# Where the fifth values and the fifth output weights travel in a decode block's stream of weights

## The chip, the cores and the metric

One core of a Trainium2 chip runs the whole program. The time is the device time of one execution, in microseconds; the kernel before took 214.63 us (median of 3 runs, 214.52 to 214.64).

## The reference

The program computes one decode step of a transformer block for a batch of B = 4 tokens of width D = 448, in float32:

```python
x_n = layernorm(x)                                   # (4, 448)
q = x_n @ wq                                         # 16 heads of 256
# 8 key/value groups, 2 heads each; the last W = 1024 cached positions
p = softmax(q . k_cache[:, g, -1024:, :] / 16)       # per token and head
o = p . v_cache[:, g, -1024:, :]
h = x + o.reshape(4, 4096) @ wo
y = layernorm(h)
out = h + gelu(y @ w1 + b1) @ w2 + b2                # w1: 448 x 1792
```

Keys and values of a group are 4 MB each, the query and output weights of a group 0.9 MB each, w1 and w2 3.2 MB each: about 88 MB that are read once, with little arithmetic on each byte.

## The kernel before, in words

**The stream.** Everything large is read by DMAs that SP issues into a ring of three slots of SBUF (pool `ring`, line 72). The list `LOADS` (lines 40 to 53) says what lies in each load, in order: quarters of keys and of values (2048 columns of 128 partitions each), query weights and output weights (1792 columns each). A load is one DMA with one semaphore, so nothing in it can be used before all of it has landed, and its slot is free for the load three places later when its last reader is done. `part` (line 89) issues the next load when a piece that isn't there yet is asked for. Behind the twelve loads come values 7 in two DMAs (`load_v7`, line 123), output weights 6 and 7, w1 and w2 (lines 351 to 360), in slots of the same ring. The program is written so that SP waits for slots, not for PE's place in the program.

**A group.** For group g of 8, `project_q` (line 196) makes the queries: products into PSUM, a copy to SBUF by ACT, and then products that both transpose and fold the four partition quadrants, since the four chunks of the contraction stand in four quadrants (`sel` has a one for each; two copies by DVE spread the result into `qT`). `scores` (214) multiplies queries and keys and takes the softmax's maximum (DVE) and exponentials (ACT). `transpose_p` (242) transposes the weights, and `values` (254) multiplies them with the values, a quarter at a time: 8 PE records of the 32. `heads` (274) scales the result, half on DVE and then half on ACT, transposes it and picks the rows of the two heads (`rows_of_pair`), and `project_o` (293) multiplies with the output weights. Groups 0 to 5 add up in one PSUM bank `acc`; for the last two groups the sum continues in `hsum` in another layout, which starts with products of a copy `accs` of `acc` (lines 342 to 349).

**The order.** PE's instructions run in the order in which they are written (line 525); the other engines are ordered by the framework. In the loop (331 to 372) the scores of group g+1 and the queries of g+2 come ahead of the values of group g. `keep_warm(n)` (322) issues n products of zeros in bfloat16 with 512 columns, whose result nobody reads; they stand where PE would wait.

**The tail.** Lines 392 to 458: the sum h, its two means and variances, the up projection with w1 (`pu`), GELU, the down projection with w2 (`py`), whose last two DMAs are small, and the output. The rows x, b2 and b1 that are added there come in one small DMA from ACT's queue (line 169), 16 rows of 704 values.

**Start.** The first load has query weights 0, the transposed x (16 columns) and 48 columns of zeros.

Of the kernel before, what the change touches and what calls it, by code (L numbers as in the profile page):

```python
# [8 lines left out]
F32 = mybir.dt.float32  # L9
BF16 = mybir.dt.bfloat16  # L10
AF = mybir.ActivationFunctionType
ALU = mybir.AluOpType
AX = mybir.AxisListType
PSUM = bass.MemoryType.PSUM

B, D = 4, 448
HQ, HKV, SK, DH = 16, 8, 4096, 256
REP = HQ // HKV
W = min(4096, max(256, SK // 4))
F = 1792  # L20
P = 128
H = P // 2
ND = 4
NKC = W // P
NFC = F // P
FQ = F // 4
Q = 32
GAP = Q // B
KV = 8 * B * DH
WC = 4 * D  # L30
QU = KV // 4
X0 = 64
V7A = 6 * B * DH


def parts(kind, g, quarters=range(4)):
    return [(kind, g, i) for i in quarters]
# [8 lines left out]
    [*parts("v", 2, (3,)), ("o", 2, 0), *parts("k", 4), ("q", 5, 0)],  # L46
    [*parts("v", 3), ("o", 3, 0), *parts("k", 5, (0, 1))],
    [*parts("k", 5, (2, 3)), ("q", 6, 0), *parts("v", 4)],
    [("o", 4, 0), *parts("k", 6), ("q", 7, 0)],
    [*parts("v", 5), ("o", 5, 0)],  # L50
    [*parts("k", 7)],
    [*parts("v", 6)],
]


# [13 lines left out]
def block_kernel(ctx: ExitStack, tc, rows, first, streams, v7, wo67, w1, w2, out):  # L69
    nc = tc.nc  # L70
    const = ctx.enter_context(tc.tile_pool(name="const", bufs=1))
# [38 lines left out]
    def wo_rows(t):  # L110
        return t.rearrange("p (j e) -> p j e", j=4)
# [8 lines left out]
    def load_v(g, c):  # L120
        return part("v", g, c).rearrange("p (c b d) -> p c b d", c=2, b=B)
# [32 lines left out]
        nc.vector.tensor_scalar_mul(fold[3 * Q :, j, :], sel[3 * Q :, :], 0.5 / D)  # L154
    fold = fold.rearrange("p j q -> p (j q)")
    rows_of = ident.rearrange("p (j b e) -> p j b e", j=4, b=B)[:, :, :, 0]
    rows_of_pair = ident.rearrange("p (b q) -> p q b", b=B)
    qT = [const.tile([P, 2, B, Q], F32, name=f"qT{i}") for i in range(2)]
    pT = [const.tile([P, NKC // 2, B, Q], F32, name=f"pT{i}") for i in range(2)]
    oT = [const.tile([P, 4, Q], F32, name=f"oT{i}") for i in range(2)]  # L160
# [3 lines left out]
    for t in qT + oT + pT + [gT]:  # L164
        nc.gpsimd.memset(t, 0.0)

    rs = const.tile([P, 2 * P + FQ], F32, name="rs")
    nc.gpsimd.memset(rs, 0.0)
    nc.scalar.dma_start(rs[::GAP, :], rows)

    def spread(t):
        return t[..., ::GAP]
    xb, b2b, b1b = rs[:, :P], rs[:, P : 2 * P], rs[:, 2 * P :]


    def column_mean(t, name):
# [19 lines left out]
    def project_q(g, parts):  # L196
        pq = ps_m.tile([P, 512], F32, tag="m", name=f"pq{g}")
        for j, a, cols, w in parts:
            nc.tensor.matmul(pq[j * Q : (j + 1) * Q, cols], yT[:, a, :], w, start=True, stop=True)  # L199
        qs = work.tile([P, 512], F32, tag="qs", name=f"qs{g}")  # L200
        nc.scalar.copy(qs, pq)  # L201

        pt = ps_m.tile([P, 512], F32, tag="m", name=f"pqt{g}")
        if g == HKV - 1:
            keep_warm(3, pt)
        pt = pt[:, : 2 * REP * B].rearrange("p (a b) -> p a b", b=B)
        for i in range(2 * REP):
            nc.tensor.matmul(pt[:, i, :], qs[:, i * P : (i + 1) * P], sel[:, :B], start=True, stop=True)  # L208

        src = pt.rearrange("p (r c) b -> p c b r", r=REP)  # L210
        for i in range(2):
            nc.vector.tensor_copy(qT[g % 2][:, :, :, i * REP : (i + 1) * REP], src)  # L212

    def scores(g):
        s = [ps_s.tile([P, 512], F32, tag="s", name=f"s{g}_{h}") for h in range(2)]
        if g == HKV - 1:
            keep_warm(12, s[0])
        mx = work.tile([P, 2], F32, tag="mx", name=f"mx{g}")
        for h in range(2):
            for c in range(2):  # L220
                for b in range(B):
                    nc.tensor.matmul(  # L222
                        s[h][b * Q : (b + 1) * Q, :], qT[g % 2][:, c, b, :], load_k(g, h, c)[:, b, :],
                        start=(c == 0), stop=(c == 1),
                    )
            nc.vector.reduce_max(mx[:, h : h + 1], s[h], axis=AX.X)  # L226
        nm = work.tile([P, 1], F32, tag="nm", name=f"nm{g}")
        nc.vector.tensor_max(nm, mx[:, 0:1], mx[:, 1:2])
        nc.vector.tensor_scalar_mul(nm, nm, -SCALE)  # L229
        p = work.tile([P, 2 * 512], F32, tag="p", name=f"p{g}")  # L230
        sums = work.tile([P, 2], F32, tag="sums", name=f"sums{g}")
        for h in range(2):
            nc.scalar.activation(  # L233
                p[:, h * 512 : (h + 1) * 512], s[h], AF.Exp, bias=nm, scale=SCALE,
                accum_out=sums[:, h : h + 1],
            )
        rec = work.tile([P, 1], F32, tag="rec", name=f"rec{g}")
        nc.vector.tensor_add(rec, sums[:, 0:1], sums[:, 1:2])
        nc.vector.reciprocal(rec, rec)
        return p, rec  # L240
# [13 lines left out]
    def values(g, v7=None):  # L254
        po = ps_o.tile([P, 2, DH], F32, tag="o", name=f"po{g}")
        for c in range(NKC // 2):
            vt = load_v(g, c) if v7 is None else v7[c]
            for b in range(B):
                nc.tensor.matmul(  # L259
                    po[b * Q : (b + 1) * Q], pT[g % 2][:, c, b, :], vt[:, :, b, :],  # L260
                    start=(c == 0), stop=(c == NKC // 2 - 1),
                )
        return po
# [5 lines left out]
    def columns(t, j):  # L269
        if j < 3:  # L270
            return t[:, j * P : (j + 1) * P].rearrange("p (i c) -> p i c", i=2)
        return t[:, None, 3 * P :].to_broadcast([t.shape[0], 2, H])

    def heads(g, po, rec):
        o = work.tile([P, 2, DH], F32, tag="o", name=f"o{g}")
        nc.vector.tensor_scalar_mul(o[:, :, :P], po[:, :, :P], rec)  # L276
        nc.scalar.mul(o[:, :, P:], po[:, :, P:], rec)  # L277
        pt = ps_m.tile([P, 512], F32, tag="m", name=f"pot{g}")
        if g >= HKV - 3:
            keep_warm(3, pt)  # L280
        pt = pt[:, : 2 * REP * B].rearrange("p (c r b) -> p c r b", c=2, r=REP)
        for c in range(2):
            for i in range(2):
                nc.tensor.matmul(  # L284
                    pt[:, c], o[:, i, c * P : (c + 1) * P], rows_of_pair[:, i * REP : (i + 1) * REP, :],
                    start=(i == 0), stop=(i == 1),
                )
        if g >= HKV - 2:
            keep_warm(1)
        dst = oT[g % 2].rearrange("p (r c) q -> p c r q", r=REP)  # L290
        nc.vector.tensor_copy(spread(dst), pt)  # L291

    def project_o(g, wt):
        for i in range(4):
# [22 lines left out]
    nc.vector.tensor_mul(yT[H:, 4, :B], d[H:, 3, :], rx[H:, :])  # L317
    project_q(0, wq_parts(t0[:, :WC]))

    tail = []  # L320

    def keep_warm(n, to=None):
        to = tail[0][:, 0, :] if to is None else to
        for _ in range(n):
            nc.tensor.matmul(to[:Q, :512], idle[:, :Q], idle, start=True, stop=True)  # L325
# [5 lines left out]
    for g in range(HKV):  # L331
        if g + 1 < HKV:
            p, rec_next = scores(g + 1)
            if g + 2 < HKV:
                project_q(g + 2, wq_parts(part("q", g + 2)))
            transpose_p(g + 1, p)
            if g + 1 == HKV - 2:
                keep_warm(8, ps_m.tile([P, 512], F32, tag="m", name="wait"))
            if g + 1 == HKV - 1:
                keep_warm(2, ps_m.tile([P, 512], F32, tag="m", name="wait"))  # L340
                tail.append(ps_t.tile([P, 2, 512], F32, tag="t", name="tail"))
                accs = once.tile([P, D], F32, tag="u", name="accs")
                nc.scalar.copy(accs, acc)
                keep_warm(8)
                hsum = ps_s.tile([P, 512], F32, tag="s", name="hsum")[:, :P]
                ph = hsum.rearrange("p (i c) -> p i c", i=2)
                pu = ps_s.tile([P, 512], F32, tag="s", name="pu")[:, :FQ]
                for j in range(4):
                    nc.tensor.matmul(ph[j * Q : (j + 1) * Q], sel, columns(accs, j), start=True, stop=False)
        else:  # L350
            v7t = load_v7()
            tw = slot("w1")
            wo_last = [wo_rows(tw[:, i * WC : (i + 1) * WC]) for i in range(2)]
            nc.sync.dma_start(tw[:, : 2 * WC], wo67)
            tw1 = tw[:, 2 * WC : 2 * WC + W1C]
            for a, n in ((0, 2 * F), (2 * F, W1C - 2 * F)):
                nc.sync.dma_start(tw1[:, a : a + n], w1[:, a : a + n])
            tw2 = slot("w2")
            for c0, n in ((0, 8), (8, 3), (11, 2), (13, 1)):
                nc.sync.dma_start(tw2[:, c0 * D : (c0 + n) * D], w2[:, c0 * D : (c0 + n) * D])  # L360
        if g == HKV - 1:
            keep_warm(6)
        po = values(g, v7t if g == HKV - 1 else None)
        heads(g, po, rec)
        if g < HKV - 2:
            project_o(g, wo_rows(part("o", g)))
        if g == HKV - 1:
            keep_warm(3)
            for i in range(2):
                project_o(HKV - 2 + i, wo_last[i])  # L370
        if g + 1 < HKV:
            rec = rec_next
# [158 lines left out]
```

## Time and profile before

| | us |
|---|---|
| median of 3 runs | 214.63 (214.52 to 214.64) |
| the profiled execution | 214.54 |
| its span, first to last instruction | 212.8 |
| PE busy | 151.3 (71%) |
| PE weight loads busy | 66.6 (31%) |
| DVE busy | 33.5 (16%) |
| ACT busy | 24.0 (11%) |
| DMA mean rate over the span | 416 GB/s, 88.52 MB |
| mean granted TensorE clock | 0.856 |

The profile is of one execution. Busy shares are averages over the whole span; PE's records are pipelined and their ends modelled, so that a start tells more than a duration. A float32 product in the normal mode stands as two records and a transpose as one. In a row of the timeline the bracket is the idle time of that engine before the row and what ended it. The clock is the share of full speed that TensorE was granted: 1.00 is 2.4 GHz, 0.50 is 1.2 GHz.

### The profile page before, as it was taken

Reading aid. Unit: us, or ns where it says so; the run is one execution under the profiler, and the core shown is the slowest. Engines: PE = TensorE matmul, PEld = TensorE weight load, DVE = VectorE, ACT = ScalarE, POOL = GpSimd, SP = SyncE. Lnnn points to the kernel's source line nnn. Section 1 sums busy time; section 2 is a strip of 40 time slices with the busy share of each in tenths; the row PEclk is TensorE's granted clock in tenths of the full one; section 3 lists DMA queues with packets and bytes.
Section 4 is the critical chain, followed back from the end, with each engine's and each line's share of the span. In section 5 each row is a group of like instructions: output and inputs, shape, how many; then the busy total and the mean of one; then the engine's idle time right before and its main releaser. Section 6 shows DMA issues by size and latency. Waiting matters only on the chain.

```text
span 212.8 us, 2636 instructions
## 1 busy us (share of the span) xinstructions
PE 151.3 (71%) x1153; PEld 66.6 (31%) x1153; DVE 33.5 (16%) x138; ACT 24.0 (11%) x57; POOL 5.6 (3%) x17
## 2 busy tenths in 40 slices
PE   0476825842894896870798770687999999999994
PEld 0342311410421622330324130143352434436443
DVE  1410310400103001310104020031130031101230
ACT  1110200300002100210003000030030102000310
POOL 6100000000000000000000000000000000000110
PEclk9999985995558569997559996589699999999999
DMA  7899797999989899998999999999999999999992
GB/s 299 376 473 508 339 508 339 501 393 449 489 357 473 381 466 430 416 481 356 487 402 445 445 405 470 434 425 384 443 409 444 416 437 425 413 411 422 429 389 72
DMA packets 3355, 88.52 MB, mean 416 GB/s; under 512 B 384, under 2 KB 640, under 8 KB 1040
## 3 DMA queue, kind: packets, MB, share of 16 engines
q1 hardware_dynamic: 3312, 88.31, 96.9%
q8 instruction: 9, 0.15, 0.3%
q10 hardware_dynamic: 32, 0.05, 0.1%
q14 instruction: 2, 0.02, 0.0%
HBM read 88.29 MB, written 0.07 MB: 415 GB/s over the span
## 4 chain that ended last, share of the span: by engine, by line
DMA 79%; PE 17%; SPq 1%; DVE 1%; issue 0%
DMA stream<-stream 68%; DMA w<-w 11%; PE s L222 8%; PE po L259 4%; PE acc L296 2%; PE pot L284 2%; PE pq L199 1%; PE py L453 0%; DVE o L276 0%; SPq L97 0%; SPq L360 0%; DVE oT L291 0%; SPq L95 0%; DVE res L457 0%
## 5 line engine op out<-in xcount | busy, mean ns | idle before, releaser
L222 PE MATMUL s<-stream,qT 128*32 128x512 f32 x256 | 41.3, 796 | 18.5 <-DMA stream<-stream 18.5
L259 PE MATMUL po<-stream,pT 128*32 128x512 f32 x224 | 30.0, 675 | 16.0 <-DMA stream<-stream 16.0
L222 PEld LDWEIGHTS s<-stream,qT 128*32 128x32 f32 x256 | 10.6, 142 | 46.2 <-issue 33.8
L226 DVE TENSOR_REDUCE mx<-s 128x1 f32<-128x512 f32 x16 | 11.1, 692 | 64.1 <-PE s L222 64.1
L259 PEld LDWEIGHTS po<-stream,pT 128*32 128x32 f32 x224 | 6.8, 119 | 33.0 <-DMA stream<-stream 18.8
L199 PE MATMUL pq<-stream,yT 128*32 128x512 f32 (+1 forms) x80 | 10.7, 630 | 5.9 <-DMA stream<-stream 3.0
L208 PE MATMUL pqt<-sel,qs 128*128 128x4 f32 x64 | 10.1, 281 | 5.5 <-ACT qs L201 5.5
L201 ACT COPY qs<-pq 128x512 f32<-128x512 f32 x8 | 4.7, 585 | 77.5 <-PE pq L199 77.5
L284 PEld LDWEIGHTS pot<-ident,o 128*128 128x128 f32 x64 | 9.8, 225 | 10.9 <-DVE o L276 10.7
L284 PE MATMUL pot<-ident,o 128*128 128x8 f32 x64 | 10.8, 287 | 3.0 <-DVE o L276 3.0
L233 ACT ACTIVATE p<-s,nm 128x512 f32<-128x512 f32 x16 | 10.9, 688 | 17.7 <-DVE nm L229 17.7
L208 PEld LDWEIGHTS pqt<-sel,qs 128*128 128x128 f32 x64 | 9.4, 226 | 10.1 <-ACT qs L201 10.1
L276 DVE TENSOR_SCALAR o<-po,rec 128x256 f32<-128x256 f32 x8 | 3.9, 484 | 53.7 <-PE po L259 53.7
L277 ACT ACTIVATE o<-po,rec 128x256 f32<-128x256 f32 x8 | 3.8, 473 | 69.3 <-DVE o L276 69.3
L325 PEld LDWEIGHTS <-idle 128*32 128x32 bf16 x77 | 6.7, 96 | 10.2 <-issue 4.4
L247 PE MATMUL ppt<-ident,p 128*128 128x128 f32 x64 | 9.8, 299 | 0.0
L296 PE MATMUL acc<-stream,oT 128*32 128x448 f32 x48 | 7.5, 701 | 2.3 <-DVE oT L291 1.4
L199 PEld LDWEIGHTS pq<-stream,yT 128*32 128x32 f32 x80 | 4.4, 128 | 13.8 <-issue 12.8
L325 PE MATMUL tail<-idle 128*32 128x512 bf16 x33 | 8.5, 381 | 0.0
L247 PEld LDWEIGHTS ppt<-ident,p 128*128 128x128 f32 x64 | 8.1, 162 | 0.9 <-ACT p L233 0.7
L193 POOL TENSOR_TENSOR r<-ve_r,mhalf 128x1 f32<-128x1 f32 x2 | 1.1, 546 | 192.0 <-DVE ve_r L192 192.0
L212 DVE COPY qT<-pqt 128x16 f32<-128x16 f32 x16 | 2.0, 170 | 18.9 <-PE pqt L208 18.9
(99 smaller groups left out, 72.5 us busy)
## 6 DMA issues: line engine op xcount, KB each, us to landing
stream<-stream SPq DMA_DIRECT2D x5, 7040.0 KB, 40.4
stream<-stream SPq DMA_DIRECT2D x2, 6912.0 KB, 39.7
stream<-stream SPq DMA_DIRECT2D x2, 4992.0 KB, 25.1
stream<-stream SPq DMA_DIRECT2D x2, 4096.0 KB, 24.1
stream<-stream SPq DMA_DIRECT2D x1, 5888.0 KB, 34.4
w<-w SPq DMA_DIRECT2D x2, 1792.0 KB, 23.1
v<-v SPq DMA_DIRECT2D x1, 3072.0 KB, 20.0
w<-wo SPq DMA_DIRECT2D x1, 1792.0 KB, 20.1
```

The source lines that it names most:

```text
L199: nc.tensor.matmul(pq[j * Q : (j + 1) * Q, cols], yT[:, a, :], w, start=True, stop=True)
L201: nc.scalar.copy(qs, pq)
L208: nc.tensor.matmul(pt[:, i, :], qs[:, i * P : (i + 1) * P], sel[:, :B], start=True, stop=True)
L222: nc.tensor.matmul(s[h][b * Q : (b + 1) * Q, :], qT[g % 2][:, c, b, :], load_k(g, h, c)[:, b, :], start=(c == 0), stop=(c == 1),)
L226: nc.vector.reduce_max(mx[:, h : h + 1], s[h], axis=AX.X)
L233: nc.scalar.activation(p[:, h * 512 : (h + 1) * 512], s[h], AF.Exp, bias=nm, scale=SCALE, accum_out=sums[:, h : h + 1],)
L247: nc.tensor.transpose(pt[:, c, :], p[:, c * P : (c + 1) * P], ident)
L259: nc.tensor.matmul(po[b * Q : (b + 1) * Q], pT[g % 2][:, c, b, :], vt[:, :, b, :], start=(c == 0), stop=(c == NKC // 2 - 1),)
L276: nc.vector.tensor_scalar_mul(o[:, :, :P], po[:, :, :P], rec)
L284: nc.tensor.matmul(pt[:, c], o[:, i, c * P : (c + 1) * P], rows_of_pair[:, i * REP : (i + 1) * REP, :], start=(i == 0), stop=(i == 1),)
L296: nc.tensor.matmul(acc[i * Q : (i + 1) * Q, :], oT[g % 2][:, i, :], wt[:, i, :], start=(g == 0), stop=(g == HKV - 3),)
L325: nc.tensor.matmul(to[:Q, :512], idle[:, :Q], idle, start=True, stop=True)
```

## The change

Four things change together.

- **Loads.** The first quarter of values 5 goes to the end of the load with output weights 4, keys 6 and query weights 7. The other three quarters go into one load with keys 7. Output weights 5 come behind values 6. There are eleven loads for twelve, with the same bytes; the largest has 14336 columns for 14080.
- **PE's order with it.** Between the first and the second quarter of values 5 stand 28 keep-warm products. Output projection 5 moves from behind heads 5 to behind values 6, ahead of heads 6, and the copy `accs` with the first products of `hsum` from ahead of values 6 to behind heads 6. Other keep-warm runs change: 12 to 4 ahead of scores 7, 8 gone ahead of values 5, 6 to 4 ahead of values 7, 3 gone in heads 6, 3 to 5 ahead of the last output projections.
- **Parity sums.** In `project_q` and `heads` the products with `sel` and `rows_of_pair` become plain transposes with `ident`, and the sum over the quadrants (or over the two heads' halves) is a `tensor_reduce` on DVE that reads PSUM.
- **Small rows.** x and b1 are no longer read as rows. b1 comes transposed in 16 columns of the first load, in place of the zeros (32 columns behind the weights instead of 64); x and b1 are brought into rows on the chip with five transposes and some copies behind `project_q(0)`. b2 alone is read as rows, in two DMAs of 64 columns.

```diff
-X0 = 64
+X0 = 2 * ND * B
 ...
-    [("o", 4, 0), *parts("k", 6), ("q", 7, 0)],
-    [*parts("v", 5), ("o", 5, 0)],
-    [*parts("k", 7)],
-    [*parts("v", 6)],
+    [("o", 4, 0), *parts("k", 6), ("q", 7, 0), *parts("v", 5, (0,))],
+    [*parts("v", 5, (1, 2, 3)), *parts("k", 7)],
+    [*parts("v", 6), ("o", 5, 0)],
...
-    rs = const.tile([P, 2 * P + FQ], F32, name="rs")
-    nc.gpsimd.memset(rs, 0.0)
-    nc.scalar.dma_start(rs[::GAP, :], rows)
+    b2b = const.tile([P, P], F32, name="b2b")
+    nc.gpsimd.memset(b2b, 0.0)
+    for cols in (slice(0, H), slice(H, P)):
+        nc.scalar.dma_start(b2b[::GAP, cols], rows[:, cols])
+    rs = const.tile([P, P + FQ], F32, name="rs")
...
         for i in range(2 * REP):
-            nc.tensor.matmul(pt[:, i, :], qs[:, i * P : (i + 1) * P], sel[:, :B], start=True, stop=True)
+            nc.tensor.transpose(pt[:, i * P : (i + 1) * P], qs[:, i * P : (i + 1) * P], ident)
+        q = work.tile([P, 2 * REP, B], F32, tag="q", name=f"q{g}")
+        quadrants = pt.rearrange("p (i j q) -> p i q j", i=2 * REP, j=4)
+        nc.vector.tensor_reduce(q, quadrants[:, :, :B, :], axis=AX.X, op=ALU.add)
...
         if g == HKV - 1:
-            keep_warm(12, s[0])
+            keep_warm(4, s[0])
...
         for c in range(NKC // 2):
+            if g == HKV - 3 and c == 1:
+                keep_warm(28, ps_m.tile([P, 512], F32, tag="m", name="wait"))
...
-        if g >= HKV - 3:
+        if g in (HKV - 3, HKV - 1):
             keep_warm(3, pt)
...
-                nc.tensor.matmul(
-                    pt[:, c], o[:, i, c * P : (c + 1) * P], rows_of_pair[:, i * REP : (i + 1) * REP, :],
-                    start=(i == 0), stop=(i == 1),
-                )
+                at = (2 * i + c) * P - i * REP
+                nc.tensor.transpose(pt[:, at : at + P], o[:, i, c * P : (c + 1) * P], ident)
...
-        nc.vector.tensor_copy(spread(dst), pt)
+        dst = oT[g % 2].rearrange("p (r c) (b e) -> p r (c b) e", r=REP, b=B)[..., 0]
+        src = pt.rearrange("p (i k q) -> p q k i", i=2, q=Q)[:, :REP]
+        nc.vector.tensor_reduce(dst, src, axis=AX.X, op=ALU.add)
...
+    nc.vector.tensor_copy(spread(zT), xT)
+    b1s = work.tile([P, 2 * 512], F32, tag="p", name="b1s")[:, : 4 * P]
+    nc.vector.tensor_copy(
+        b1s.rearrange("p (c j q) -> p c j q", c=4, j=4), b1T[:, :, :, None].to_broadcast([P, 4, 4, Q])
+    )
+    pb = ps_s.tile([P, 512], F32, tag="s", name="pb")
+    for c in range(3):
+        nc.tensor.transpose(pb[:, c * P : (c + 1) * P], b1s[:, c * P : (c + 1) * P], ident)
+    nc.tensor.transpose(pb[:, 3 * P : FQ], b1s[:H, 3 * P :], ident[:H, :H])
+    nc.scalar.copy(b1b, pb[:, :FQ])
+    px = ps_s.tile([P, 512], F32, tag="s", name="px")
+    nc.tensor.transpose(px[:, :P], zT.rearrange("p j q -> p (j q)"), ident)
+    nc.vector.tensor_copy(xb, px[:, :P])
...
-            if g + 1 == HKV - 2:
-                keep_warm(8, ps_m.tile([P, 512], F32, tag="m", name="wait"))
             if g + 1 == HKV - 1:
                 keep_warm(2, ps_m.tile([P, 512], F32, tag="m", name="wait"))
                 tail.append(ps_t.tile([P, 2, 512], F32, tag="t", name="tail"))
-                accs = ... hsum = ... pu = ...      # to behind heads 6
                 keep_warm(8)
...
         if g == HKV - 1:
-            keep_warm(6)
+            keep_warm(4)
         po = values(g, v7t if g == HKV - 1 else None)
+        if g == HKV - 2:
+            project_o(g - 1, wo_rows(part("o", g - 1)))
         heads(g, po, rec)
-        if g < HKV - 2:
+        if g < HKV - 3:
             project_o(g, wo_rows(part("o", g)))
+        if g == HKV - 2:
+            accs = ... hsum = ... pu = ...
         if g == HKV - 1:
-            keep_warm(3)
+            keep_warm(5)
```

## Rows read from the trace of the kernel before

**Rows 1.** The page's chain of work that ended last: shares of the span by engine

```profile
DMA 79%; PE 17%; SPq 1%; DVE 1%; issue 0%
```

**Rows 2.** A stretch: window, length, busy by engine, granted clock, DMA share, GB/s

```profile
2.00:209.00 207.00, 150.36 (x1132) 66.06 (x1132) 32.37 (x131) 24.04 (x57) 4.15 (x8) 0.85 1.00 427
```

**Rows 3.** Timeline of SP's queue: start, us from first issue to last, line, target

```profile
25.05 0.33 SPq L97 DMA_DIRECT2D stream<-stream  x1
...
146.41 10.01 SPq L97 DMA_DIRECT2D stream<-stream  x2
167.53 0.80 SPq L126 DMA_DIRECT2D v<-v  x2
...
183.97 3.90 SPq L360 DMA_DIRECT2D w<-w  x4
```

**Rows 4.** Timeline of PE and its weight loads, where a load is awaited

```profile
118.39 1.92 PE L259 MATMUL po<-stream,pT 128*32 128x512 f32 x16 [1.10 <-DMA stream<-stream]
...
135.04 3.64 PE L222 MATMUL s<-stream,qT 128*32 128x512 f32 x16 [8.27 <-DMA stream<-stream]
...
149.07 1.16 PE L296 MATMUL acc<-stream,oT 128*32 128x448 f32 x8 [0.94 <-DMA stream<-stream]
...
160.80 3.64 PE L259 MATMUL po<-stream,pT 128*32 128x512 f32 x32 [0.18 <-DMA stream<-stream]
...
170.53 3.64 PE L222 MATMUL s<-stream,qT 128*32 128x512 f32 x32 [0.49 <-DMA stream<-stream]
...
180.26 3.64 PE L259 MATMUL po<-stream,pT 128*32 128x512 f32 x32 [0.18 <-DMA stream<-stream]
...
194.35 1.95 PE L302 MATMUL hsum<-w,oT 128*32 128x128 f32 x64 [0.31 <-DMA w<-wo]
...
201.89 0.16 PEld L422 LDWEIGHTS pu<-w,zT 128*32 128x32 f32 x8 [0.23 <-DMA w<-w]
...
208.98 0.37 PEld L453 LDWEIGHTS py<-w,gT 128*32 128x32 f32 x16 [0.34 <-DMA w<-w]
209.56 0.16 PEld L453 LDWEIGHTS py<-w,gT 128*32 128x32 f32 x8 [0.21 <-DMA w<-w]
```

**Rows 5.** Timeline of PE at the first scores

```profile
17.64 6.48 PE L222 MATMUL s<-stream,qT 128*32 128x512 f32 x32 [1.83 <-DMA stream<-stream]
```

**Rows 6.** Stretches, columns as in rows 2, after two waits of PE

```profile
135.00:140.00 5.00, 4.95 (x26) 1.34 (x26) 1.01 (x3) 0.00 (x0) 0.00 (x0) 0.55 1.05 452
...
150.00:152.00 2.00, 2.00 (x16) 0.75 (x12) 0.00 (x0) 0.00 (x0) 0.00 (x0) 0.50 0.74 319
152.00:154.00 2.00, 2.00 (x16) 0.59 (x12) 0.50 (x1) 0.00 (x0) 0.00 (x0) 0.72 1.07 459
```

**Rows 7.** Timeline, group 6's transposed weights, and what follows values 5

```profile
157.70 1.09 PE L247 MATMUL ppt<-ident,p 128*128 128x128 f32 x8
...
158.83 0.29 DVE L251 COPY pT<-ppt 128x32 f32<-128x32 f32 x2 [0.36 <-PE ppt L247]
...
164.26 0.81 PE L325 MATMUL pot<-idle 128*32 128x512 bf16 x3
```

**Rows 8.** Timeline, output projection 5, copy of the sums, scaling in heads 7

```profile
166.51 0.96 PE L296 MATMUL acc<-stream,oT 128*32 128x448 f32 x8 [0.28 <-DVE oT L291]
...
167.28 2.75 PE L325 MATMUL s<-idle 128*32 128x512 bf16 x12
167.53 0.53 ACT L343 COPY accs<-acc 128x448 f32<-128x448 f32 x1 [1.97 <-PE acc L296]
...
191.36 0.48 DVE L276 TENSOR_SCALAR o<-po,rec 128x256 f32<-128x256 f32 x1 [5.45 <-PE po L259]
...
191.94 0.47 ACT L277 ACTIVATE o<-po,rec 128x256 f32<-128x256 f32 x1 [6.91 <-DVE o L276]
```

**Rows 9.** Timeline, keep-warm products between scores 7 and values 6

```profile
173.99 2.32 PE L325 MATMUL ppt<-idle 128*32 128x512 bf16 x10
...
177.96 1.68 PE L325 MATMUL tail<-idle 128*32 128x512 bf16 x7
```

More of the change, by code (lines that the diff above doesn't have):

```diff
@@ L156, in block_kernel @@
     rows_of = ident.rearrange("p (j b e) -> p j b e", j=4, b=B)[:, :, :, 0]
-    rows_of_pair = ident.rearrange("p (b q) -> p q b", b=B)
     qT = [const.tile([P, 2, B, Q], F32, name=f"qT{i}") for i in range(2)]
@@ L165, in block_kernel @@
         nc.gpsimd.memset(t, 0.0)
-    rs = const.tile([P, 2 * P + FQ], F32, name="rs")
-    nc.gpsimd.memset(rs, 0.0)
-    nc.scalar.dma_start(rs[::GAP, :], rows)
+    b2b = const.tile([P, P], F32, name="b2b")
[3 more added lines that the diff above has]
+    rs = const.tile([P, P + FQ], F32, name="rs")
     def spread(t):
         return t[..., ::GAP]
-    xb, b2b, b1b = rs[:, :P], rs[:, P : 2 * P], rs[:, 2 * P :]
+    xb, b1b = rs[:, :P], rs[:, P:]
     def column_mean(t, name):
@@ L205, in project_q @@
             keep_warm(3, pt)
-        pt = pt[:, : 2 * REP * B].rearrange("p (a b) -> p a b", b=B)
         for i in range(2 * REP):
-            nc.tensor.matmul(pt[:, i, :], qs[:, i * P : (i + 1) * P], sel[:, :B], start=True, stop=True)
-        src = pt.rearrange("p (r c) b -> p c b r", r=REP)
+            nc.tensor.transpose(pt[:, i * P : (i + 1) * P], qs[:, i * P : (i + 1) * P], ident)
+        q = work.tile([P, 2 * REP, B], F32, tag="q", name=f"q{g}")
+        quadrants = pt.rearrange("p (i j q) -> p i q j", i=2 * REP, j=4)
+        nc.vector.tensor_reduce(q, quadrants[:, :, :B, :], axis=AX.X, op=ALU.add)
+        src = q.rearrange("p (r c) b -> p c b r", r=REP)
         for i in range(2):
@@ L278, in heads @@
         pt = ps_m.tile([P, 512], F32, tag="m", name=f"pot{g}")
-        if g >= HKV - 3:
+        if g in (HKV - 3, HKV - 1):
             keep_warm(3, pt)
-        pt = pt[:, : 2 * REP * B].rearrange("p (c r b) -> p c r b", c=2, r=REP)
         for c in range(2):
             for i in range(2):
-                nc.tensor.matmul(
-                    pt[:, c], o[:, i, c * P : (c + 1) * P], rows_of_pair[:, i * REP : (i + 1) * REP, :],
-                    start=(i == 0), stop=(i == 1),
-                )
+                at = (2 * i + c) * P - i * REP
+                nc.tensor.transpose(pt[:, at : at + P], o[:, i, c * P : (c + 1) * P], ident)
         if g >= HKV - 2:
             keep_warm(1)
-        dst = oT[g % 2].rearrange("p (r c) q -> p c r q", r=REP)
-        nc.vector.tensor_copy(spread(dst), pt)
+        dst = oT[g % 2].rearrange("p (r c) (b e) -> p r (c b) e", r=REP, b=B)[..., 0]
+        src = pt.rearrange("p (i k q) -> p q k i", i=2, q=Q)[:, :REP]
+        nc.vector.tensor_reduce(dst, src, axis=AX.X, op=ALU.add)
     def project_o(g, wt):
@@ L318, in block_kernel @@
     project_q(0, wq_parts(t0[:, :WC]))
+    b1T = t0[:, WC + ND * B :].rearrange("p (c j) -> p c j", c=4)
+    nc.vector.tensor_copy(spread(zT), xT)
[11 more added lines that the diff above has]
+    nc.vector.tensor_copy(xb, px[:, :P])
     tail = []
@@ L341, in block_kernel @@
                 tail.append(ps_t.tile([P, 2, 512], F32, tag="t", name="tail"))
-                accs = once.tile([P, D], F32, tag="u", name="accs")
-                nc.scalar.copy(accs, acc)
                 keep_warm(8)
[L345 to L349, printed above, removed]
         else:
@@ L361, in block_kernel @@
         if g == HKV - 1:
-            keep_warm(6)
+            keep_warm(4)
         po = values(g, v7t if g == HKV - 1 else None)
+        if g == HKV - 2:
+            project_o(g - 1, wo_rows(part("o", g - 1)))
         heads(g, po, rec)
-        if g < HKV - 2:
+        if g < HKV - 3:
             project_o(g, wo_rows(part("o", g)))
+        if g == HKV - 2:
+            accs = once.tile([P, D], F32, tag="u", name="accs")
+            nc.scalar.copy(accs, acc)
+            hsum = ps_s.tile([P, 512], F32, tag="s", name="hsum")[:, :P]
+            ph = hsum.rearrange("p (i c) -> p i c", i=2)
+            pu = ps_s.tile([P, 512], F32, tag="s", name="pu")[:, :FQ]
+            for j in range(4):
+                nc.tensor.matmul(ph[j * Q : (j + 1) * Q], sel, columns(accs, j), start=True, stop=False)
         if g == HKV - 1:
-            keep_warm(3)
+            keep_warm(5)
             for i in range(2):
@@ L487 @@
     wo = np.asarray(A_wo).reshape(HKV, 4, P, D).transpose(0, 2, 1, 3).reshape(HKV, P, 4 * D)
-    first = np.concatenate([wq[0], xT, np.zeros((P, X0 - ND * B), np.float32)], axis=1)
+    b1 = np.zeros((4, 4 * P), np.float32)
+    b1[:, :FQ] = np.asarray(B_b1).reshape(4, FQ)
+    first = np.concatenate([wq[0], xT, b1.reshape(4, 4, P).transpose(2, 1, 0).reshape(P, 16)], axis=1)
     def part(kind, g, i):
@@ L511 @@
     b2 = np.concatenate([b2, b2[:, 3 * P :]], axis=1)
-    rows = np.concatenate([quadrants(xp), quadrants(b2), quadrants(np.asarray(B_b1).reshape(1, F))], axis=2)
-    rows = rows.reshape(4 * B, -1)
+    rows = quadrants(b2).reshape(4 * B, -1)
     arrays = {
```

## The prediction

> **What bounds the kernel now.** I read four views. First the chain of waits: the shares by engine put 79% on transfers [rows 1]; the reader should see that PE appears only as the piece between two transfers. Next the stretches: from 2 to 209 us the DMA engines are busy all the time (share 1.00) at 427 GB/s [rows 2]. So the end is set by the bytes, as long as the queue never runs dry. Third the SP queue: the late loads are issued over 10 us before the one ahead of them is through (146.41 for one whose turn comes near 160.8, 167.53 for one whose turn comes near 180.3) [rows 3, 4], so a few us of later slot release cost nothing. Last the timeline of PE, for where PE waits for a transfer and how long, since that is the slack that the change can eat [rows 4]: 0.18 us ahead of the values of group 6 (180.26), 0.31 ahead of the last output projection (194.35), 0.23 in the up projection (201.89), 0.34 and 0.21 in the down projection (208.98, 209.56). PE is thus nearly as late as the transfers all along the last 40 us. What matters is whether the new order makes PE later than they are.
>
> **The transfers.** The rows shrink from 16x704 to 16x128 values and the first load by 32 columns: 36.9 KB and 16.4 KB, 53 KB at 427 GB/s, 0.12 us less. One load fewer: 8192 columns take 9.73 us (160.80 to 170.53, 170.53 to 180.26) and 14080 take 16.65 (118.39 to 135.04) [rows 4]; 1.175 ns a column and 0.1 us a load solve both, PE's own lag included, so I allow 0 to 0.1 and take 0.03. The stream ends 0.15 us earlier, and if it still set the end the profiled execution would take 214.4 for its 214.54.
> The order within it: the ninth load gets a quarter of values 5, 2048 columns, 2.43 us by the rate above, so output weights 4 and keys 6 are seen at 149.07 + 2.43 - 0.12 = 151.4. Keys 7 now come with the rest of values 5 and without output weights 5 (1792 columns, 2.13 us): 170.53 - 2.13 - 0.12 = 168.3 for both. Values 6 with output weights 5 land at 180.1, as values 6 alone did.
> The Trainium skill prices a load otherwise. "DMA: Bandwidth & Descriptors" (Anatomy of one DMA) fits a fixed cost of about 2 us to each DMA; if that stood in the stream, one load fewer would bring 2 us. The 9.73 and 16.65 us show at most a tenth of it between queued loads.
>
> **The start.** Five transposes, a broadcast copy and three copies are added before the first scores, some 2.5 us of PE, DVE and ACT by their nearest rows (eight transposes 1.09, a copy 0.15 to 0.53 [rows 7, 8]). PE waits 1.83 us for keys 0 there [rows 5], which hides most of it. Uncovered, up to 1 us, it would delay the release of the first slot from 25.05 [rows 3], when two more loads of 16.65 each are queued: nothing.
>
> **The parity sums.** In every group four products of two passes become four one-pass transposes (half of the 1.09 of eight [rows 7]) and a copy becomes a DVE sum over 32 or 64 values, which no row shows. Its bounds are 0.15 (one of the two copies of 128x32, 0.29 together [rows 7]) and 0.48 (DVE's 128x256 [rows 8]); I take 0.25. Through group 4 this lies ahead of waits for loads. In the tail the transposes are in the sum below, and the sum on DVE ends, at 0.48 too, under the keep-warm products that follow.
>
> **PE from 151.4.** Before, PE goes from output projection 4 (149.07) to the transposed weights of group 6 (158.83 + 0.29 [rows 7]) in 10.1 us. Now the first quarter of values 5 follows (8 of 32 products; 32 free PE after 164.26 - 160.80 = 3.46, so 0.86), and 28 keep-warm products at 0.216 ((2.32 - 0.38)/9 [rows 9]), 6.05. From 151.4 this ends at 168.4, beside the landing at 168.3. But PE has then been idle for 3.8 us (the 0.94 of before [rows 4], 2.3 for the later load, 0.55 for the shorter transposes of heads 4), and the clock counts: after 149.07 it was granted 0.50 until about 153, after the pause of 8.27 before 135.04 it was granted 0.55 on average up to 140 [rows 6], that is the low level of 1.2 GHz for 4.4 us. Low stretches of 3 to 6 us after work resumes cost 0.5 less to 1 us more than the 2 us lost before. I take 0.3 more: values 5 go on at 168.7 (bounds 168.3, when the landing decides, and 169.4).
>
> **From there to the last output projection, all on PE's path:**
> - three quarters of values 5: 3.71 from first product to DVE's scaling (160.80; scaling 3.71 after it as 0.25 after PE is free), less 0.86: 2.85.
> - heads 5: DVE 0.48, then ACT 0.47, which starts 0.58 after DVE (191.36, 191.94 [rows 8]), then two transposes; PE is free 1.45 after DVE's start. Four keep-warm products 0.87. Scores 7 start at 168.7 + 5.2 = 173.9, where they started at 170.53: moving the values in front of them costs 3.4.
> - scores 7 to values 6: 170.53 to 177.96 [rows 4, 9] and eight keep-warm products, 9.16: values 6 at 183.0, the load long there (180.1).
> - values 6, output projection 5 (0.77, from 166.51 to 167.28 [rows 8]), heads 6, ACT's copy of the sums 0.53 [rows 8], which ACT runs after its half of heads 6, eight small products 0.54 and four keep-warm ones: 3.71 + 0.58 + 0.47 + 0.6 + 0.6 + 0.87 = 6.8. Values 7 at 189.8. (Output projection 5 lies under DVE's and ACT's scaling.) The copy of the sums and its products were done before beside a wait for a load; here PE waits for them.
> - values 7: 3.71, and heads 7 with one and five keep-warm products: 1.45 + 1.30. The last output projection starts at 196.3, where it started at 194.35: 1.95 later.
>
> **What the tail gives back.** After 194.35 PE waits 0.23 and 0.55 for weights [rows 4]; these 0.78 absorb part. The end comes 1.95 - 0.78 = 1.2 us later: 215.7 for 214.54. With the landing deciding at 168.3 it is 0.8 (215.3), with the clock's upper bound 1.9 (216.4). The median of the runs shown is 0.09 above the profiled execution, less than the working resolves; I put the time at 215.7.
> The queue doesn't add to this: the last values 7 are issued near 163 (the slot goes with the first quarter of values 5), w1 near 178 against a queue filled until 190, w2 near 188, 4 us later than at 183.97 [rows 3], against one filled until 201.9.
>
> **The rivals.**
> 1. Transfers still set the end: 214.4, not slower. The place is the last output projection; it decides if that starts by 195.1, that is if my 27.6 us from 168.7 are 1.2 too many, or 0.8 from 168.3. For it: every keep-warm run is filler, and two of the heads' steps rest on one overlap each that I read from single rows. Against: each of the six pieces is a row of the same shape.
> 2. A second low stretch of the clock between 184 and 195, where three keep-warm products of heads 6 and two-pass products are gone and PE waits for ACT twice. At the 3 us of the stretch after 150 [rows 6] half is lost, 1.5 us more: 217.2. Against: project and keep-warm products still fill most of it.
> The Trainium skill speaks for this one: "TensorE: Matmul & The Clock Gate" (Part 4: PE-mode transpose) says that transposes don't count as busy for the clock as matmuls do. No row before shows transposes alone; the eight at 157.70 stand at full clock among other work [rows 7].
> 3. Faster: rival 1's short PE path, 0.12 for the bytes, 0.1 for the load, and a stream whose other sizes run 0.2% quicker (0.4 us of 207): 213.9. Nothing in the rows points to the last. By the fixed cost that the Trainium skill's DMA page states it would be 212.5; the two spacings leave that next to nothing, and I count it within this rival.
>
> **How the numbers follow.** My forecast 0.60, rival 1 0.24, rival 2 0.11, rival 3 0.05. 0.2% (0.43 us) is about what a measurement of this kernel can tell from no change. Forecast and rival 2 are slower by more than that, but for the edge of the forecast's lower bound (0.02 taken off); rival 1 lies within it save for 0.04 on the fast side, so faster 0.09, same 0.22, slower 0.69. The range runs from rival 1 (214.3) to the forecast's upper bound and part of rival 2, 217.0; the forecast's own is 215.2 to 216.5.
>
> **What would show it.** Right: in the changed profile no PE wait for a transfer between 170 and the down projection; scores 7 start near 173.9, values 6 near 183, the last output projection near 196.3; the down projection runs through without a wait for weights while the last transfer lands near 209.4. Wrong: PE waiting for w2 at the end, as now; or the output projection on time because keys 7 and values 5 are seen well before 168.

## The result and the profile after

The changed kernel takes 215.06 us (median of 13 runs, 214.77 to 215.72) and the kernel before 214.59 (13 runs beside them, 214.44 to 214.75): a ratio of 1.0028, 95% interval 1.0021 to 1.0036. It is slower, by 0.5 us where 1.2 was forecast. The profiled execution took 215.35, with a span of 213.5; against the 214.54 of before that is 0.81 more. The runs spread over 0.95 us, those of before over 0.31.

The chain of waits, shares by engine, in the changed kernel (against [rows 1]):

```profile
DMA 59%; PE 35%; DVE 1%; ACT 1%; issue 1%; SPq 1%; ACTq 0%
```

PE's share has doubled. The same view in order of time (start, length, what) shows where:

```profile
112.24 38.85 DMA stream<-stream
151.23 1.72 PE acc L298 x8
152.95 5.08 PE s L224 x32
...
161.67 1.00 PE po L263 x8
162.66 5.81 PE wait L343 x27
168.47 2.85 PE po L263 x21
171.35 0.49 DVE o L280
171.93 0.48 ACT o L281
...
177.29 2.16 PE ppt L343 x10
...
207.52 3.30 PE py L472 x66
```

After the load with output weights 4, at 151.23, no transfer stands on the chain any more: it is PE's work, its keep-warm products among it, with short steps of DVE and ACT, to the down projection. In [rows 4] PE waited for a load at 160.80, 170.53, 180.26, 194.35, 201.89, 208.98 and 209.56; none of these waits is left.

The steps of the sum, in the timeline of PE, ACT and DVE in the changed kernel (where three records of a group stand ahead of the last keep-warm product and the rest behind it, I count from the start of the longer row):

```profile
168.52 1.94 PE L263 MATMUL po<-stream,pT 128*32 128x512 f32 x16
...
173.70 3.60 PE L224 MATMUL s<-stream,qT 128*32 128x512 f32 x29
...
182.85 3.60 PE L263 MATMUL po<-stream,pT 128*32 128x512 f32 x29
...
187.11 0.47 ACT L281 ACTIVATE o<-po,rec 128x256 f32<-128x256 f32 x1 [7.09 <-DVE o L280]
...
187.48 0.52 ACT L380 COPY accs<-acc 128x448 f32<-128x448 f32 x1
188.01 0.39 PE L343 MATMUL tail<-idle 128*32 128x512 bf16 x1
188.07 0.55 PE L385 MATMUL hsum<-accs,sel 128*32 128x128 f32 x8
...
188.45 0.81 PE L343 MATMUL tail<-idle 128*32 128x512 bf16 x3
...
189.31 3.60 PE L263 MATMUL po<-v,pT 128*32 128x512 f32 x29
...
195.78 1.91 PE L304 MATMUL hsum<-w,oT 128*32 128x128 f32 x58
...
197.78 0.29 DVE L414 SCALAR_TENSOR_TENSOR h<-hsum,rs 128x128 f32<-128x128 f32 x1 [3.00 <-PE hsum L304]
...
207.52 3.26 PE L472 MATMUL py<-w,gT 128*32 128x128 f32 x112 [0.39 <-issue]
210.84 0.29 DVE L476 TENSOR_TENSOR res<-py,hb 128x128 f32<-128x128 f32 x1 [3.20 <-PE py L472]
```

The reader should see the last row but one: 112 records of the down projection in one piece, with no wait for w2 in it. The same places of the tail in the kernel before:

```profile
196.37 0.29 DVE L395 SCALAR_TENSOR_TENSOR h<-hsum,rs 128x128 f32<-128x128 f32 x1 [3.07 <-PE hsum L302]
...
206.31 3.68 PE L453 MATMUL py<-w,gT 128*32 128x128 f32 x112 [0.39 <-DVE gT L445]
210.06 0.29 DVE L457 TENSOR_TENSOR res<-py,hb 128x128 f32<-128x128 f32 x1 [3.63 <-PE py L453]
```

And the stretches around the pause (columns as in [rows 2]):

```profile
148.00:150.00 2.00, 0.00 (x0) 0.00 (x0) 0.00 (x0) 0.00 (x0) 0.00 (x0) 0.83 1.05 455
150.00:152.00 2.00, 0.77 (x8) 0.29 (x12) 0.00 (x0) 0.00 (x0) 0.00 (x0) 0.50 1.06 459
...
154.00:156.00 2.00, 2.00 (x12) 0.46 (x8) 0.00 (x0) 0.00 (x0) 0.00 (x0) 0.50 1.06 459
156.00:158.00 2.00, 2.00 (x24) 0.70 (x20) 0.69 (x1) 0.00 (x0) 0.00 (x0) 0.97 0.96 410
158.00:196.00 38.00, 37.47 (x277) 15.68 (x266) 6.43 (x24) 5.22 (x13) 0.00 (x0) 1.00 0.98 418
```

The clock fell to 1.2 GHz in PE's pause ahead of 151.23, stayed there for 4.9 us of work, and was full from 156.1 to the end.

### The profile page after: what moved, and what is told of

Read it like the earlier page. It is cut to its first block, busy times and chain, and to the rows that moved or that the text cites. A ratio compares the mean times of both kernels' runs of the same rounds, so it can differ in the third digit from the quotient of the medians.

```text
span 213.5 us, 2547 instructions
## 1 busy us (share of the span) xinstructions
PE 148.9 (70%) x1103; PEld 58.4 (27%) x1103; DVE 36.2 (17%) x149; ACT 24.5 (11%) x58; POOL 5.1 (2%) x17
## 4 chain that ended last, share of the span: by engine, by line
DMA 59%; PE 35%; DVE 1%; ACT 1%; issue 1%; SPq 1%; ACTq 0%
DMA stream<-stream 59%; PE po L263 8%; PE s L224 8%; PE tail L343 3%; PE wait L343 3%; PE acc L298 2%; PE pot L288 2%; PE pu L441 2%; PE py L472 2%; PE ppt L249 1%; DVE o L280 1%; PE ppt L343 1%; PE hsum L304 1%; PE pq L199 1%; ACT o L281 1%
## 5 line engine op out<-in xcount | busy, mean ns | idle before, releaser
L263 PE MATMUL po<-stream,pT 128*32 128x512 f32 x224 | 31.2, 681 | 14.9 <-DMA stream<-stream 14.9
L263 PEld LDWEIGHTS po<-stream,pT 128*32 128x32 f32 x224 | 7.5, 120 | 30.9 <-DMA stream<-stream 16.9
L298 PE MATMUL acc<-stream,oT 128*32 128x448 f32 x48 | 8.4, 750 | 4.7 <-DMA stream<-stream 3.6
L249 PE MATMUL ppt<-ident,p 128*128 128x128 f32 x64 | 11.1, 303 | 0.2
L343 PEld LDWEIGHTS <-idle 128*32 128x32 bf16 x86 | 7.7, 96 | 11.3 <-issue 4.3
L288 PE MATMUL pot<-ident,o 128*128 128x128 f32 x32 | 7.7, 338 | 3.7 <-DVE o L280 3.1
L207 PE MATMUL pqt<-ident,qs 128*128 128x128 f32 x32 | 6.1, 323 | 5.6 <-ACT qs L201 5.6
L288 PEld LDWEIGHTS pot<-ident,o 128*128 128x128 f32 x32 | 3.6, 156 | 13.5 <-DVE o L280 10.9
L343 PE MATMUL wait<-idle 128*32 128x512 bf16 x30 | 6.8, 379 | 0.0
L207 PEld LDWEIGHTS pqt<-ident,qs 128*128 128x128 f32 x32 | 3.9, 159 | 10.2 <-ACT qs L201 8.5
```

The source lines that it names most:

```text
L207: nc.tensor.transpose(pt[:, i * P : (i + 1) * P], qs[:, i * P : (i + 1) * P], ident)
L249: nc.tensor.transpose(pt[:, c, :], p[:, c * P : (c + 1) * P], ident)
L263: nc.tensor.matmul(po[b * Q : (b + 1) * Q], pT[g % 2][:, c, b, :], vt[:, :, b, :], start=(c == 0), stop=(c == NKC // 2 - 1),)
L288: nc.tensor.transpose(pt[:, at : at + P], o[:, i, c * P : (c + 1) * P], ident)
L298: nc.tensor.matmul(acc[i * Q : (i + 1) * Q, :], oT[g % 2][:, i, :], wt[:, i, :], start=(g == 0), stop=(g == HKV - 3),)
```

## The experiments

Theory A is that of the prediction: the new order puts PE behind the transfers. Theory B: the sums on DVE, the transposes or the start cost the time. Theory C: the clock does. Ratios are to the kernel before, measured beside each.

**The parts apart.** e1 is the changed kernel with the loads, the order and the keep-warm runs of before:

```diff
-    [("o", 4, 0), *parts("k", 6), ("q", 7, 0), *parts("v", 5, (0,))],
-    [*parts("v", 5, (1, 2, 3)), *parts("k", 7)],
-    [*parts("v", 6), ("o", 5, 0)],
+    [("o", 4, 0), *parts("k", 6), ("q", 7, 0)],
+    [*parts("v", 5), ("o", 5, 0)],
+    [*parts("k", 7)],
+    [*parts("v", 6)],
...
```

> The parity sums and the small rows as in the changed kernel, with the loads, PE's order and the keep-warm runs of the kernel before. Theory A (the order makes PE late): the transfers set the end again, 0.15 us earlier than before, so a ratio to before of 0.999 (214.4), with PE waiting for the last piece of w2. Theory B (the sums, the DVE work or the start cost the time): 1.002 to 1.003 (215.1), as the changed kernel.

Measured: 214.44 (11 runs), 0.9995 (0.9987 to 1.0004). PE's weight loads wait for transfers again:

```profile
194.22 1.69 PEld L303 LDWEIGHTS hsum<-w,oT 128*32 128x32 f32 x64 [0.96 <-DMA w<-wo]
201.76 0.16 PEld L439 LDWEIGHTS pu<-w,zT 128*32 128x32 f32 x8 [0.23 <-DMA w<-w]
...
209.44 0.16 PEld L470 LDWEIGHTS py<-w,gT 128*32 128x32 f32 x8 [0.19 <-DMA w<-w]
```

The last piece of w2 is seen at 209.44 for 209.56, so the smaller rows and first load do save 0.1 us of stream. The sums, the transposes and the start alone do not slow the kernel: B falls.

e2 is the kernel before with the new loads, order and keep-warm runs alone, the opposite edit:

```diff
-    [("o", 4, 0), *parts("k", 6), ("q", 7, 0)],
+    [("o", 4, 0), *parts("k", 6), ("q", 7, 0), *parts("v", 5, (0,))],
...
+            if g == HKV - 3 and c == 1:
+                keep_warm(28, ps_m.tile([P, 512], F32, tag="m", name="wait"))
...
```

> The loads, PE's order and the keep-warm runs of the changed kernel, with the products by sel and rows_of_pair and the small rows of the kernel before. Theory A: slower than the changed kernel too, because heads 5, 6 and 7 keep two more records each on PE's path (0.22 each) and the stream is 0.12 later: 1.005 (215.7). Theory B: no slower than before, 1.000.

Measured: 215.69 (6 runs), 1.0059 (1.0047 to 1.0071), as A expects. The loads and the order cost 1.2 us by themselves; the sums and rows then give 0.6 back. Most of that is the transposes, which shorten the heads on a path that PE now sets: in e2's profile values 5 to scores 7, values 6 to values 7 and values 7 to the last output projection take 5.37, 6.64 and 6.64 us, in the changed kernel's 5.18, 6.46 and 6.47. In e1, where the transfers set the end, only the bytes saved could count.

**Filler on PE's path.** By filler I mean keep-warm products. e3 leaves out ten keep-warm products, e5 adds ten, at the same place ahead of values 6:

```diff
-                keep_warm(2, ps_m.tile([P, 512], F32, tag="m", name="wait"))
                 tail.append(ps_t.tile([P, 2, 512], F32, tag="t", name="tail"))
-                keep_warm(8)          # e3; in e5: 2 and 18
```

> The changed kernel without the ten keep-warm products between scores 7 and values 6. Theory A: they lie on PE's path, so the last output projection could start 2.16 us earlier (193.6) and waits for its weights again (landing 194.0); the transfers set the end: 0.9985 (214.3). Theory C (the clock): without filler the granted clock falls to 0.5 somewhere after 180 and the time is above 215.5 (1.004 or more).

> The changed kernel with ten more keep-warm products (18 for 8) ahead of values 6. Theory A: PE's path has no slack left behind them, so all of 10 x 0.216 shows at the end: 215.06 + 2.16 = 217.2 (ratio 1.0125), and the transfers land when they did. If the transfers or the waits for them set the end: 215.1 (1.003).

Measured: e3 214.27 (11 runs), 0.9988 (0.9979 to 0.9996); e5 217.98 (4 runs), 1.0163 (1.0147 to 1.0178). In e3 the waits for weights are back, the clock stays at 1.00 from 158 to 196 (no sign of C), and the last landings are the end:

```profile
194.07 1.69 PEld L304 LDWEIGHTS hsum<-w,oT 128*32 128x32 f32 x64 [0.54 <-DMA w<-wo]
...
209.28 0.16 PEld L470 LDWEIGHTS py<-w,gT 128*32 128x32 f32 x8 [0.20 <-DMA w<-w]
```

e5 came 0.8 over its expected 217.2. Its timeline says where:

```profile
169.00 2.74 PE L263 MATMUL po<-stream,pT 128*32 128x512 f32 x21
...
185.47 3.60 PE L263 MATMUL po<-stream,pT 128*32 128x512 f32 x29
...
198.41 1.91 PE L304 MATMUL hsum<-w,oT 128*32 128x128 f32 x58
```

Values 5 went on at 169.00 instead of 168.52, 0.48 later before the added products come; from there to values 6 it is 16.47 for 14.33, the ten products and next to nothing else. So against the profiled 215.35 it is 2.16 and 0.48, 217.99. The low stretch after 151 ended at 157.0 here, in the changed kernel's profile at 156.1. The four runs stood together there (217.92 to 218.19), above the longest run of the changed kernel with 2.16 added (217.88); why all four came out that late is not shown.

**The common landing.** e6 loads three quarters of values 5 and keys 7 as two DMAs into the same slot, and moves filler from values 5 to places where PE then waits:

```diff
+            if wanted[0] == ("v", 5, 1):
+                nc.sync.dma_start(t[:, : 3 * QU], src[:, : 3 * QU])
+                nc.sync.dma_start(t[:, 3 * QU : src.shape[-1]], src[:, 3 * QU :])
...
-                keep_warm(28, ps_m.tile([P, 512], F32, tag="m", name="wait"))
```

> The changed kernel with its ninth-but-one load (three quarters of values 5, then keys 7) as two DMAs into the same slot, each with its own semaphore, and the 28 keep-warm products taken out of values 5 (4 more ahead of scores 7, 10 more ahead of values 6, where PE now waits). Theory A: it is the common landing that makes PE late, so values 5 run through at 161.7, scores 7 start when keys 7 land (168.1, for 173.7), values 6 wait for their load (179.9), and the transfers set the end: 0.9985 (214.3). If the place of output projection 5 and of the copied sums is what costs: not below 1.002.

Measured: 214.47 (11 runs), 0.9996 (0.9988 to 1.0005). PE is back in time everywhere:

```profile
160.31 3.64 PE L265 MATMUL po<-stream,pT 128*32 128x512 f32 x32
...
168.03 3.64 PE L228 MATMUL s<-stream,qT 128*32 128x512 f32 x32 [0.64 <-DMA stream<-stream]
...
179.87 3.64 PE L265 MATMUL po<-stream,pT 128*32 128x512 f32 x32 [0.34 <-DMA stream<-stream]
...
193.97 1.95 PE L306 MATMUL hsum<-w,oT 128*32 128x128 f32 x64
```

Scores 7 start at 168.03 instead of 173.70, with output projection 5 and the copied sums where the change put them. The cause is that values 5 wait for keys 7 and scores 7 then wait for values 5. The 28 products taken out are not what held values 5: in e10 (below), with 12 of them, PE still waits for the load, over 5 us.

```profile
168.13 4.07 PE L263 MATMUL po<-stream,pT 128*32 128x512 f32 x24 [5.03 <-DMA stream<-stream]
```

**The copied sums.** In e11 the four products of `accs` (eight records, which the prediction and the expectation call eight products) come behind values 7, the copy itself where it was.

```diff
         po = values(g, v7t if g == HKV - 1 else None)
+        if g == HKV - 1:
+            hsum = ...; pu = ...
+            for j in range(4): nc.tensor.matmul(ph[...], sel, columns(accs, j), start=True, stop=False)
```

> The changed kernel with its eight products of the copied sums behind values 7 instead of ahead of them, so that PE doesn't wait for ACT's copy. Theory A: values 7 start 0.43 us earlier (the time from 188.0 to 188.4 in which PE issues them and waits), all on the path: 215.06 - 0.4 = 214.65 (1.0007). If the wait is hidden: 215.06 (1.0025).

Measured: 214.78 (11 runs, 214.61 to 215.59), 1.0012 (1.0004 to 1.0021), 0.3 of the expected 0.4 below the changed kernel's median. The intervals of the two just touch, and the profile gives the price:

```profile
182.53 3.60 PE L263 MATMUL po<-stream,pT 128*32 128x512 f32 x29
...
188.78 3.60 PE L263 MATMUL po<-v,pT 128*32 128x512 f32 x29
```

Values 6 to values 7 take 6.25 us for the changed kernel's 6.46: these products lay on the path and cost 0.21, half of the 0.43 expected. The rest of what this execution gained (214.82 for 215.35) was there before values 6, which start 0.32 sooner.

**The clock.** e4 fills PE's pause ahead of output projection 4; e9 is the same kernel again; e8 has 36 products for 28 in values 5 besides, e10 has 12.

```diff
+        if g == HKV - 4:
+            keep_warm(16, ps_m.tile([P, 512], F32, tag="m", name="wait"))
         if g < HKV - 3:
             project_o(g, wo_rows(part("o", g)))
...
             if g == HKV - 3 and c == 1:
-                keep_warm(28, ps_m.tile([P, 512], F32, tag="m", name="wait"))
+                keep_warm(36, ps_m.tile([P, 512], F32, tag="m", name="wait"))   # e8; e10: 12; e4, e9: 28
```

> The changed kernel with 16 keep-warm products in PE's pause of 3.6 us ahead of output projection 4. Theory A with the clock as its cause of spread: the clock stays at 1.0 through scores 6, the 28 keep-warm products end near 166, and values 5 go on when their load lands (168.1) in every run: 1.0015 (214.9), with a spread of 0.4 us where the changed kernel has 0.95. If the low clock after that pause plays no part: 1.0028 and the same spread.

Measured: 215.55 (7 runs), 1.0044 (1.0025 to 1.0063), and the spread grew to 1.55: three runs at 214.83 to 214.93, four at 215.55 to 216.38. The profiled execution took 214.92 as expected, but the expectation had no price for the pause of 1.56 us that PE then makes ahead of the landing at 168.1:

```profile
168.09 2.78 PE L263 MATMUL po<-stream,pT 128*32 128x512 f32 x24 [1.56 <-DMA stream<-stream]
```

Hence three more:

> The kernel with the filled pause once more, for another profile: if this execution takes 215.5 or more, a stretch of clock 0.50 between 168 and 196 (about 1 to 1.7 us lost) shows it; if it takes 214.9, the clock is 1.00 there.

> The pause ahead of output projection 4 filled as in the run before, and 36 keep-warm products for 28 in values 5, so that PE doesn't pause ahead of the landing at 168.1 either. Theory A with the clock as cause of the spread: the runs of the other kernel at 215.5 to 216.4 fell to a low clock after its pause of 1.6 us at 166.5; without a pause every run is near its best, 214.9 (1.0018), spread under 0.4. If the spread has another cause: 215.5 again, spread above 1.

> As the kernel with the filled pause, but with 12 keep-warm products for 28 in values 5, so that PE pauses for about 5 us ahead of the landing at 168.1 in every execution. If the clock makes the long runs of that kernel: the granted clock falls to 0.50 in this pause and stays there for 1.5 to 5 us of values 5 and heads 5, half of which shows at the end: 215.6 to 217.3 in every run, none at 214.9. If something else makes them: 214.9 in most runs again.

Measured: e9 214.99 (8 runs; five at 214.85 to 215.00, three at 215.97 to 216.53), 1.0043 (1.0023 to 1.0063), its profile again of one of the short ones. e8 214.92 (11 runs, 214.82 to 215.09), 1.0019 (1.0010 to 1.0028). e10 216.53 (4 runs, 216.26 to 217.04), 1.0099 (1.0084 to 1.0115). The stretches of e10, and then one of e8:

```profile
164.00:166.00 2.00, 0.00 (x0) 0.00 (x0) 0.00 (x0) 0.00 (x0) 0.00 (x0) 1.00 0.82 352
166.00:168.00 2.00, 0.00 (x0) 0.00 (x0) 0.00 (x0) 0.00 (x0) 0.00 (x0) 0.84 0.84 359
168.00:170.00 2.00, 1.87 (x12) 0.57 (x16) 0.00 (x0) 0.00 (x0) 0.00 (x0) 0.50 1.02 439
170.00:172.00 2.00, 2.00 (x20) 0.41 (x13) 0.00 (x0) 0.00 (x0) 0.00 (x0) 0.81 1.11 479
```

```profile
148.00:196.00 48.00, 47.22 (x352) 19.55 (x351) 7.12 (x25) 5.23 (x13) 0.00 (x0) 1.00 0.99 425
```

In e10 the clock is at 1.2 GHz from the end of the pause to about 170.8, for 2.6 us of values 5, half of which is 1.3, and its profiled execution is 1.34 over e4's (216.26 and 214.92). In e8 PE is busy almost without a gap, the clock is 1.00 from 148 to 196, and the spread is 0.27. So the pause is what brings the long runs of e4 and e9. That it does so by this low clock is what e10 makes likely, and not shown: no profile caught a long run, and the mean clocks on record, over whole executions, do not tell the two kinds apart (0.879 to 0.889 in the seven long runs, 0.880 to 0.888 in the eight others).

e8 also answers C for the change itself: without any low stretch between 148 and 196 the kernel still takes 1.0019 of the one before, so the low clock alone does not make it slower, though it may add to it.

## Why the prediction was right, and where it was off

- **Bound and mechanism: right.** With the stream as the end, e1, e3 and e6 stand at 214.27 to 214.47 (forecast 214.4); with the new order PE sets it. Rival 1 (not slower) did not happen, because the slack that [rows 4] show behind the last output projection is 0.78 us and PE came 1.4 late to it. The 215.06 lies in the range, but just under the 215.2 to 216.5 that the prediction gave to this forecast alone: the mechanism is the forecast's, but two of its steps were taken too long (below).
- **The transfers: right.** Output weights 4 were seen at 151.23 (forecast 151.4), keys 7 with values 5 at 168.1 in e4, e9 and e10, where PE waits for them (168.3).
- **The start and the parity sums: right.** PE still waits 0.85 us for keys 0; the DVE sums took 0.19 (32 values) and 0.22 (64 values), for the 0.25 taken and the copies' 0.19.
- **Values 5 to scores 7 and on to values 6: right.** 168.52 to 173.70 is 5.18 (forecast 5.2), 173.70 to 182.85 is 9.15 (9.16), values 7 to the last output projection 6.47 (6.46).
- **Start of values 5: off by 0.2** in the profiled execution (168.5 for 168.7). The allowance for the clock was of the right kind. Four profiles are of the same code up to there: with the clock full again at 155.4 (e3), 155.5 (e11), 156.1 (the changed kernel) and 157.0 (e5), values 5 went on at 168.14, 168.06, 168.52 and 169.00, the first two at the landing. e8, without the low stretch, stands at 214.92 where the bound with the landing deciding said 215.3.
- **Values 6 to values 7: mis-sized, with a wait that was not there.** I took 6.8, it was 6.46 (182.85 to 189.31). The prediction has PE wait for ACT's copy of the sums. The copy begins at 187.48, ahead of the end of the scaling's row (187.11 + 0.47), and is done at 188.00; PE comes to the keep-warm product ahead of the eight records of `hsum` at 188.01, so it does not wait. These eight cost 0.21 (e11), where the sum has 0.6 for them. This and the start make the last output projection 1.43 late (195.78) for 1.95.
- **What the tail gives back: mis-sized.** 1.41 us at the sum h (197.78 for 196.37) became 0.78 at the output (210.84 for 210.06): 0.63 given back for 0.78. The 0.23 of the up projection gave 0.21 (203.09 for 201.89), the 0.55 of the down projection only 0.42: without its two waits its row shrinks from 3.68 to 3.26, so not all of the idle time in such a bracket was lost.
- **Together** 1.43 - 0.63 = 0.8 in the profiled execution, for a forecast of 1.2; its 215.35 lies 0.29 over the median. A low stretch longer than in most runs would explain that; the other runs have no profile, so it is not shown.
- **Rival 2 (a second low stretch): did not happen.** The clock was 1.00 from 158 to 196. By the Trainium skill, "TensorE: Matmul & The Clock Gate" (Part 4: PE-mode transpose), transposes do not count as busy for the clock the way matmuls do. The trace does not contradict it: among other work they did no harm, and no run here shows them alone.
- **Rival 3: did not happen.** By the Trainium skill's "DMA: Bandwidth & Descriptors" (Anatomy of one DMA) one DMA less would be worth about 2 us, an estimate from a fit that the page gives for DMAs issued by GpSimd. For the loads that SP queues here the traces show nothing of the kind: e6 and e1 each have one load more than e3, and their last piece of w2 is seen 0.10 us earlier and 0.16 later (209.18 and 209.44 for 209.28).

## What to carry to other kernels

Where transfers set the end, as here before the change, list for each wait of the compute engine how long it is, and treat any reordering as spending that slack: here 0.8 us were there behind the last output projection and 1.4 were spent. Two pieces in one DMA share one landing, so put together only what is used together; splitting the load, or dropping filler that had come to lie on the path, removed the whole loss. e3 is the shortest here, 0.9988 (0.9979 to 0.9996) of the kernel before.

## What the runs showed that I had not expected

Filling one pause opened another. With PE earlier and 1.56 us of waiting ahead of 168.1, 7 of 15 runs (e4 and e9) came out 0.6 to 1.7 us longer than the others, while both profiled executions of that kernel were short ones and showed nothing. Here the short pause cost more than the filler that fills it: 36 keep-warm products in place of 28 (e8) brought every run to within 0.27 us. Ten other keep-warm products, on PE's path with no wait behind them, cost their whole 2.1 us (e5): the same filler pays in a pause and costs on the path.
